# A fused attention and expert kernel: where the second expert unit's weights are split, and in which order

## The chip, the cores and the metric

The kernel runs as one program on one core of a Trainium2 chip. The metric is the time of one execution on the device in microseconds (us); lower is better. A core has engines that run side by side, each with its own queue of instructions: TensorE (PE, with its weight loads shown as PEld) multiplies matrices, VectorE (DVE) and ScalarE (ACT) work on elements, GpSimd (POOL) here issues indirect transfers, and SyncE (SP) issues most DMAs.

## The reference

The computation has three stages on 1792 tokens of width 768, all in 32-bit floats.

```python
attn = softmax(causal(q @ k.T / 8)) @ v          # 4 batches, 12 heads, 448 tokens, width 64
h = x @ w_in;  x = (h - tanh(h)) @ w_out         # 768 -> 2048 -> 768
logits = x @ w_gate;  e = argmax(logits)         # one of 8 experts for each token
for e in range(8):
    y = relu(x[mask_e] @ w1[e]) @ w2[e]          # 768 -> 1024 -> 768
    out[mask_e] = softmax_e * sigmoid(x @ w_output_gate[:, e]) * y
```

## The kernel before

Precision comes from splitting. A 32-bit operand is held as a high part, rounded by a cast on ACT (line 83), and a low part, the rest, by a subtraction on DVE (line 84); a product is then three TensorE products (high by high, low by high, high by low) that add up in PSUM.

The change lies in the third stage, `experts`. It works in units of 256 tokens of one expert: nine units, of which the first is the expert with the most tokens, the second is expert 0's ("early"), and the other seven follow. A unit of weights is 16 chunks of 128 x 768: eight for W1 and eight for W2. A unit runs eight *up* groups (`up`, lines 1098 to 1105: 18 products into one of three PSUM buffers named h, then a relu on ACT, line 1104, and the low part on DVE, line 1105) and four *down* groups (`down`, lines 1118 to 1127: 24 products for half of the tokens and half of the width, then a scaling on DVE or ACT). The tokens of the next unit are transposed and split inside a unit (`split`, lines 1086 to 1089: transposes on PE into tr, the cast xh on ACT, the rest xl on DVE).

Weights come in two steps. `Supply` (line 88) has eight rooms for raw chunks; SP fetches a chunk into a room (line 107) as soon as the room has been freed by the split of the chunk that stood there. `supply.load()` (line 111) splits the next raw chunk into a slot of the `ring` (class `Weights`, line 55). The ring has 16 slots, 18 once two spare ones have been added; a slot is free when the last product that reads it is done. During the last products of the second stage eight loads fill unit 0's W1. Each up group of a unit is followed by one load, and each down group by two. Unit 0 has two more at its end. So the sixteen loads of a unit run ahead of their use: in unit 0 the up groups are followed by the loads of its own W2, the down groups by those of unit 1's W1; from unit 1 on, two chunks further.

Unit 0 also carries the end of the routing: small steps (`late`) are taken from a list between its up groups, and the last of them, which make `allids` and `allcf`, in `leave()` behind the third down group. `leave()` then closes the routing's memory and opens the pool `ring2` in its place, with the two spare slots. `add_slots` puts them at the ring's present position, so the next two loads take them: in unit 0 these are the seventh and eighth chunk of unit 1's W1. Their splits have to wait until `allcf` has been made.

The order of instructions on an engine is not that of the program: a planner orders each engine's queue by its own model of costs, before the program runs. `tc.keep_in_program_order(x)` fixes one thing, that instruction x stands behind the instruction that was written just before it for the same engine; others can still be placed between. Once ordered, each queue runs in its order.

After the units a loop would take tokens of an expert beyond the planned ones. Whether it runs is in one word, `sel[0, 1]`, made in unit 0; `values_load` (line 1180) reads it into a register of each engine, and `tc.If` (line 1181) branches on it. With these inputs the loop does not run.

Of the kernel before, what the change touches and what calls it, by code (L numbers as in the profile page):

```python
# [9 lines left out]
F32 = mybir.dt.float32  # L10
# [4 lines left out]
ALU = mybir.AluOpType  # L15
# [39 lines left out]
class Weights:  # L55
# [20 lines left out]
    def unsplit(self, i):  # L76

        pool, n = self.slots[i]
        return pool.tile([P, 768, 2], I32, tag=f"w{n}", name=f"raw{n}", bufs=1)

    def split(self, raw, a):
        t = self.slot()
        self.nc.scalar.copy(t[:, 0, :], raw)  # L83
        self.nc.vector.tensor_tensor(t[:, 1, :], raw, t[:, 0, :].bitcast(F32), op=ALU.subtract)  # L84
        return self.parts(t, a)


# [34 lines left out]
class Decoder:  # L122
# [9 lines left out]
    keep = staticmethod(lambda x: x)  # L132
# [910 lines left out]
def gather(nc, pool, x2s, ids, c0):  # L1043

    xg = []
    for t in range(2):
        x = pool.tile([P, x2s.shape[1]], F32, tag="xg", name="xg")
        nc.gpsimd.indirect_dma_start(
            out=x, out_offset=None, in_=x2s,
            in_offset=IndirectOffsetOnAxis(ap=ids[:, c0 + t:c0 + t + 1], axis=0),  # L1050
        )
        xg.append(x)
    return xg
# [8 lines left out]
def experts(tc, consts, ring, xg, early, late, route_close, w12, x2s, lst, out):  # L1062


    nc = tc.nc
# [5 lines left out]
    supply = consts["supply"]  # L1071

    ctx = ExitStack()
    sp = ctx.enter_context(tc.tile_pool(name="ex", bufs=2))
    ps = consts["rtps"]
    rows = lst.rearrange("(r b) c -> r (b c)", b=P)

    def split(xg):
        hi = sp.tile([P, KD, 2, P], F32R, tag="xh", name="xh")
        lo = sp.tile([P, KD, 2, P], F32R, tag="xl", name="xl")  # L1080
        for k in range(KD // 2):
            pt = ps.tile([P, 2, 2, P], F32, tag="tr", name="tr")
            for a in range(2):
                for t in range(2):
                    d = (2 * k + a) * P
                    nc.tensor.transpose(pt[:, a, t, :], xg[t][:, d:d + P], ident)  # L1086
            s = slice(2 * k, 2 * k + 2)
            nc.scalar.copy(hi[:, s], pt)
            nc.vector.tensor_tensor(lo[:, s], pt, hi[:, s].bitcast(F32), op=ALU.subtract)
        return hi, lo  # L1090

    def up(x, w, f):
        ph = consts["hps"].tile([P, 2 * P], F32, tag="h", name="h")
        wh, wl = w
        n = 0
        for kd in range(KD):
            for wp, a in ((wh, x[0]), (wl, x[0]), (wh, x[1])):
                nc.tensor.matmul(  # L1098
                    ph, wp[:, kd, :], a[:, kd].rearrange("p a b -> p (a b)"),
                    start=(n == 0), stop=(n == 3 * KD - 1),  # L1100
                )
                n += 1
        h = [sp.tile([P, 2 * P], F32R, tag=f"h{i}", name=f"h{i}", bufs=KF) for i in range(2)]
        nc.scalar.activation(h[0], ph, AF.Relu)
        nc.vector.scalar_tensor_tensor(  # L1105
            h[1], ph, 0.0, h[0].bitcast(F32), op0=ALU.max, op1=ALU.subtract
        )
        return h

    def down(hs, W2, y, cf, t, o):  # L1110
        hn = DM // 2
        c = slice(t * P, (t + 1) * P)
        py = ps.tile([P, hn], F32, tag="y", name="py")
        n = 0
        for f in range(KF):
            wh, wl = W2[f]
            for a, w in ((0, wh), (0, wl), (1, wh)):
                nc.tensor.matmul(  # L1118
                    py, hs[f][a][:, c], w[:, 0, o * hn:(o + 1) * hn],
                    start=(n == 0), stop=(n == 3 * KF - 1),  # L1120
                )
                n += 1
        ye = y[:, o * hn:(o + 1) * hn]
        if o == 0:
            nc.vector.tensor_scalar_mul(ye, py, cf)
        else:
            nc.scalar.mul(ye, py, cf)

    def put(y, ids):
        nc.gpsimd.indirect_dma_start(  # L1130
            out=out, out_offset=IndirectOffsetOnAxis(ap=ids, axis=0),
            in_=y, in_offset=None, bounds_check=NT - 1, oob_is_err=False,
        )

    todo = [(consts[nm + "ids"], consts[nm + "cf"], 0) for nm in ("", "early")]
    todo += [(consts["allids"], consts["allcf"], 2 * e) for e in range(1, E)]
    x = split(xg)
    late.pop(0)()

    def leave():  # L1140

        nonlocal ps
        while late:
            late.pop(0)()
        route_close()
        rp = ctx.enter_context(tc.tile_pool(name="ring2", bufs=1))
        ring.add_slots(rp, 2)
        ps = ctx.enter_context(tc.tile_pool(name="exps", bufs=2, space=PSUM))

    for u, (iu, cu, c0) in enumerate(todo):  # L1150
        nxt = todo[u + 1] if u + 1 < len(todo) else None
        if u > 0 and nxt:
            xg = gather(nc, consts["xg"], x2s, nxt[0], nxt[2])
        hs = []
        W1 = supply.take(KF)
        for f in range(KF):
            hs.append(up(x, W1[f], f))
            supply.load()
            if u == 0:
                for _ in range(LATER[f]):  # L1160
                    late.pop(0)()
        if u == 0:
            xg = early[-1]
        W2 = supply.take(KF)
        for t in range(2):
            y = sp.tile([P, DM], F32, tag="y", name="y")
            for o in range(2):
                down(hs, W2, y, cu[:, c0 + t:c0 + t + 1], t, o)
                if (t, o) == ((1, 0) if u == 0 else (0, 0)) and nxt:
                    x = split(xg)  # L1170
                for _ in range(2):
                    supply.load()
                if u == 0 and (t, o) == (1, 0):
                    leave()
            put(y, iu[:, c0 + t:c0 + t + 1])
        if u == 0:
            for _ in range(2):
                supply.load()

    more = nc.values_load(consts["sel"][0:1, 1:2], min_val=0, max_val=1)  # L1180
    with tc.If(more > 0):
        for e in range(E):
            lo = nc.values_load(consts["begin"][0:1, e:e + 1], min_val=1, max_val=2)
            hi = nc.values_load(consts["units"][0:1, e:e + 1], min_val=0, max_val=per // 2)
            with tc.For_i(lo, hi, 1) as u:
                pt = turn_list(
                    nc, ps, fetch_list(nc, sp, rows[bass.ds(e * per + 2 * u, 2), :], 2), 2, ident
                )
                iu = sp.tile([P, 2], I32, tag="iu", name="iu", bufs=1)
                cu = sp.tile([P, 2], F32, tag="cu", name="cu", bufs=1)  # L1190
                nc.vector.tensor_copy(iu, pt[:, 0, :])
                nc.vector.tensor_copy(cu, pt[:, 1, :])
                x = split(gather(nc, consts["xg"], x2s, iu, 0))
                supply.add(weight_chunks(w12[e], KD, KF))
                supply.fill()
                for _ in range(2 * KF):
                    supply.load()
                W1, W2 = supply.take(KF), supply.take(KF)
                hs = [up(x, W1[f], f) for f in range(KF)]
                for t in range(2):  # L1200
                    y = sp.tile([P, DM], F32, tag="y", name="y")
                    for o in range(2):
                        down(hs, W2, y, cu[:, t:t + 1], t, o)
                    put(y, iu[:, t:t + 1])
# [4 lines left out]
def fused(ctx, tc, qk, v, w_in, w_out, gw, gates, w12, out):  # L1209
# [34 lines left out]
    def turnover():  # L1244
# [12 lines left out]
        tc, consts, ring, last, wo, gw, gates, w12, gT, x2s, lst  # L1257
    )
    experts(tc, consts, ring, xg, early, late, close, w12, x2s, lst, out)


# [61 lines left out]
```

## Time and profile before

| what | value |
| --- | --- |
| median of 3 runs | 1026.77 us (1023.33 to 1027.82) |
| profiled execution | 1028.09 us |
| its span | 1026.4 us, 16686 instructions |
| PE busy | 997.9 us, 97% of the span |
| DVE busy | 655.3 us, 64% |
| ACT busy | 489.0 us, 48% |
| POOL busy | 78.3 us, 8% |
| granted PE clock | 0.994 of full speed on average |
| up products of the experts (L1098) | 156.8 + 122.1 us |
| down products with the high part of h (L1118) | 155.3 us |
| weight casts (L83), expert stage | x144, 113.9 us |
| weight subtractions (L84), expert stage | x144, 131.7 us |
| fetches of expert weights (L107) | x144, 384 KB each, 5.2 us median to landing |

The span runs from the first instruction to the last of the profiled execution; its time on the device is 1.7 us longer. Attention and the two dense layers take the first two thirds; unit 0's first up product is at 689.5 us, and the last down product starts at 1013.9 us. Busy shares are averages over the whole span; idle time of an engine other than PE costs nothing unless PE waits for it.

### The profile page before, as it was taken

What the parts mean: (1) busy time and instruction counts of PE and PEld (TensorE: products, weight loads), DVE (VectorE), ACT (ScalarE), POOL (GpSimd) and SP (SyncE); (2) the same over time, 40 slices, a digit from 0 to 9 for tenths busy, and PEclk for the clock granted to TensorE, in tenths of its full rate; (3) what the DMA queues carried; (4) which work ended last, traced back from release to release, by engine and by line L of the source; (5) the groups of instructions that cost most, each with busy time, mean ns of one, the idle gap of its engine ahead of it and who ended that gap; (6) DMA issues with size and microseconds to landing.
All of it is one profiled execution on the core that took longest, in us unless ns stands there. A gap on an engine that the chain in (4) does not pass through costs nothing.

```text
span 1026.4 us, 16686 instructions
## 1 busy us (share of the span) xinstructions
PE 997.9 (97%) x6174; PEld 899.4 (88%) x6174; DVE 655.3 (64%) x1453; ACT 489.0 (48%) x1021; POOL 78.3 (8%) x84
## 2 busy tenths in 40 slices
PE   8999999999999999999999999999999999999995
PEld 3566888787878888999999999989999999999995
DVE  4779997877777745426677677556566654755530
ACT  4678886676766544312121122154554543554330
POOL 1000000000000000000111121111311111011000
PEclk9999999999999999999999999999999999999998
DMA  8444746675666318544242334298567755774500
GB/s 307 133 148 123 207 149 189 199 243 183 213 198 197 116 45 255 186 168 132 88 145 87 114 88 143 74 306 278 204 242 243 248 188 185 256 237 136 178 15 32
DMA packets 89100, 176.50 MB, mean 172 GB/s; under 512 B 8818, under 2 KB 52072, under 8 KB 89010
## 3 DMA queue, kind: packets, MB, share of 16 engines
q1 hardware_dynamic: 84258, 157.37, 48.3%
q0 software_dynamic: 4304, 16.97, 5.1%
q8 instruction: 50, 0.82, 0.4%
q10 hardware_dynamic: 448, 1.02, 0.3%
q14 instruction: 40, 0.33, 0.1%
HBM read 142.81 MB, written 34.08 MB: 172 GB/s over the span
## 4 chain that ended last, share of the span: by engine, by line
PE 78%; DMA 8%; DVE 7%; ACT 3%; issue 2%; SPq 0%; POOL 0%; POOLq 0%; ACTq 0%; DVEq 0%
PE x2p L683 20%; PE h L477 15%; PE h L1098 14%; PE py L1118 14%; DMA wo<-dy 3%; PE x L445 3%; PE pt L406 3%; PE s L341 3%; PE s L350 3%; DMA glo<-gT 2%; PE warm L506 2%; PE tr L1086 1%; DMA wraw<-in_w_dram 1%; DVE pr L367 1%; DVE w L84 1%
## 5 line engine op out<-in xcount | busy, mean ns | idle before, releaser
L477 PE MATMUL h<-xh,w 128*128 128x448 f32 x768 | 228.4, 375 | 0.8 <-DVE g L491 0.6
L683 PE MATMUL x2p<-w,ghi 128*128 128x384 f32 x896 | 228.9, 336 | 0.0
L683 PEld LDWEIGHTS x2p<-w,ghi 128*128 128x128 f32 x896 | 161.0, 188 | 0.3 <-issue 0.2
L1098 PE MATMUL h<-xh,w 128*128 128x256 f32 x864 | 156.8, 284 | 3.3 <-DVE h L1105 2.0
L1118 PE MATMUL py<-w,h 128*128 128x384 f32 x864 | 155.3, 336 | 0.0
L683 PE MATMUL x2p<-w,glo 128*128 128x384 f32 x448 | 150.0, 335 | 0.0
L1118 PEld LDWEIGHTS py<-w,h 128*128 128x128 f32 x864 | 149.1, 188 | 0.0
L477 PEld LDWEIGHTS h<-xh,w 128*128 128x128 f32 x768 | 139.2, 189 | 10.0 <-DVE g L491 1.4
L84 DVE TENSOR_TENSOR w<-wraw,w 128x768 fp32r<-128x768 f32 x144 | 131.7, 953 | 21.5 <-ACT w L83 21.5
L477 PE MATMUL h<-xl,w 128*128 128x448 f32 x384 | 142.4, 373 | 0.0
L1098 PEld LDWEIGHTS h<-xh,w 128*128 128x128 f32 x864 | 134.7, 191 | 4.3 <-DVE h L1105 2.2
L83 ACT CAST w<-wraw 128x768 fp32r<-128x768 f32 x144 | 113.9, 830 | 36.1 <-PE py L1118 28.5
L1098 PE MATMUL h<-xl,w 128*128 128x256 f32 x432 | 122.1, 283 | 0.0
L376 ACT ACTIVATE pr<-pr,mx 128x128 f32<-128x128 f32 (+3 forms) x168 | 89.0, 530 | 52.8 <-DVE mx L367 49.3
L706 DVE CUSTOM_DVE_ANT_0 junk<-x,row 128x768 bf16<-128x768 f32 x88 | 84.2, 957 | 31.8 <-ACT x L692 29.6
L683 PEld LDWEIGHTS x2p<-w,glo 128*128 128x128 f32 x448 | 84.1, 188 | 0.2 <-issue 0.2
L1098 PEld LDWEIGHTS h<-xl,w 128*128 128x128 f32 x432 | 82.6, 191 | 0.4 <-issue 0.4
L367 DVE CUSTOM_DVE_ANT_0 pr<-s,mask 128x384 f32<-128x384 f32 (+2 forms) x144 | 60.1, 420 | 30.9 <-PE s L341 20.4
L477 PEld LDWEIGHTS h<-xl,w 128*128 128x128 f32 x384 | 72.3, 189 | 4.6
L406 PE MATMUL pt<-ident,pr 128*128 128x128 f32 x384 | 62.7, 276 | 0.2 <-ACT pr L389 0.2
L491 DVE TENSOR_TENSOR g<-h,g 128x448 f32<-128x448 f32 x64 | 39.6, 620 | 34.6 <-ACT g L490 34.2
L406 PEld LDWEIGHTS pt<-ident,pr 128*128 128x128 f32 x384 | 46.5, 141 | 13.5 <-issue 4.1
(178 smaller groups left out, 1174.9 us busy)
## 6 DMA issues: line engine op xcount, KB each, us to landing
wraw<-in_w_dram SPq DMA_DIRECT2D x144, 384.0 KB, 5.2
gT<-g SPq DMA_DIRECT2D x64, 224.0 KB, 2.2
glo<-gT SPq DMA_DIRECT2D x14, 1024.0 KB, 7.2
draw<-in_w_out_dram SPq DMA_DIRECT2D x16, 768.0 KB, 4.8
raw<-in_w_in_dram SPq DMA_DIRECT2D x14, 768.0 KB, 6.1
q<-in_qk_dram SPq DMA_DIRECT2D x36, 240.0 KB, 3.9
k<-in_qk_dram SPq DMA_DIRECT2D x36, 224.0 KB, 3.9
wo<-dy SPq DMA_DIRECT2D x16, 384.0 KB, 4.6
```

Source lines behind the costliest of these rows:

```text
L83: self.nc.scalar.copy(t[:, 0, :], raw)
L84: self.nc.vector.tensor_tensor(t[:, 1, :], raw, t[:, 0, :].bitcast(F32), op=ALU.subtract)
L341: nc.tensor.matmul(d, self.qh[:, o:o + P], x[:, kcol[i]:kcol[i] + w], start=(n == 0), stop=(n == last - 1),)
L367: nc.vector.tensor_tensor_reduce(out=self.probs(r), in0=ss[:, o:o + w], in1=m, scale=-0.125, scalar=3.0e38, op0=ALU.add, op1=ALU.min, accu ...
L376: nc.scalar.activation(pc, pc, AF.Exp, bias=self.mx[:, x:x + 1], scale=-1.0, accum_out=self.sm[:, x:x + 1],)
L406: nc.tensor.transpose(pt[:, n * P:(n + 1) * P], self.pr[:, o:o + P], ident)
L477: nc.tensor.matmul(ph, w[:, kd, :], x, start=(kd == 0 and n == 0), stop=(kd == KD - 1 and n == 2))
L491: nc.vector.tensor_tensor(g, ph, g, op=ALU.subtract)
L683: nc.tensor.matmul(px, a[:, f, :], w[:, 0, h * hn:(h + 1) * hn], start=(n == 0), stop=(n == 3 * NF - 1),)
L706: nc.vector.tensor_tensor_reduce(out=junk, in0=x2, in1=row, scale=1.0, scalar=0.0, op0=ALU.mult, op1=ALU.add, accum_out=to,)
L1098: nc.tensor.matmul(ph, wp[:, kd, :], a[:, kd].rearrange("p a b -> p (a b)"), start=(n == 0), stop=(n == 3 * KD - 1),)
L1118: nc.tensor.matmul(py, hs[f][a][:, c], w[:, 0, o * hn:(o + 1) * hn], start=(n == 0), stop=(n == 3 * KF - 1),)
```

## The change

There are four edits. (1) `Weights` gets a hook `keep`, and both instructions of a weight split pass through it. In units 0 and 1 it is set to `tc.keep_in_program_order` after the first up group and set back when the unit's W2 is taken, so the splits written between the up groups of these two units are pinned behind the relu and the h subtraction of the group before them. (2) The loads in the down part stand ahead of each down group instead of behind it; in unit 0 they are four ahead of each of the first two groups and none ahead of the others, where it was two behind each of four. (3) The spare slots are added to the ring after unit 0's last down group instead of in `leave()`; the pool is still opened there. So all eight W1 chunks of unit 1 take slots of unit 0's W1, and the two spare slots go to the first two chunks of unit 1's W2. (4) The word for the loop is read at the beginning of the last unit instead of behind it.

```diff
+    keep = staticmethod(lambda x: x)
+
     def split(self, raw, a):
         t = self.slot()
-        self.nc.scalar.copy(t[:, 0, :], raw)
-        self.nc.vector.tensor_tensor(t[:, 1, :], raw, t[:, 0, :].bitcast(F32), op=ALU.subtract)
+        self.keep(self.nc.scalar.copy(t[:, 0, :], raw))
+        self.keep(self.nc.vector.tensor_tensor(
+            t[:, 1, :], raw, t[:, 0, :].bitcast(F32), op=ALU.subtract
+        ))
         return self.parts(t, a)
...
         route_close()
-        rp = ctx.enter_context(tc.tile_pool(name="ring2", bufs=1))
-        ring.add_slots(rp, 2)
+        ring2 = ctx.enter_context(tc.tile_pool(name="ring2", bufs=1))
         ps = ctx.enter_context(tc.tile_pool(name="exps", bufs=2, space=PSUM))
 
     for u, (iu, cu, c0) in enumerate(todo):
+        if u == len(todo) - 1:
+            more = nc.values_load(consts["sel"][0:1, 1:2], min_val=0, max_val=1)
...
         for f in range(KF):
             hs.append(up(x, W1[f], f))
+            if u < 2:
+                ring.keep = tc.keep_in_program_order
             supply.load()
...
         W2 = supply.take(KF)
+        ring.keep = lambda x: x
         for t in range(2):
             y = sp.tile([P, DM], F32, tag="y", name="y")
             for o in range(2):
+
+                for _ in range(2 if u else 4 - 4 * t):
+                    supply.load()
                 down(hs, W2, y, cu[:, c0 + t:c0 + t + 1], t, o)
                 if (t, o) == ((1, 0) if u == 0 else (0, 0)) and nxt:
                     x = split(xg)
-                for _ in range(2):
-                    supply.load()
                 if u == 0 and (t, o) == (1, 0):
                     leave()
             put(y, iu[:, c0 + t:c0 + t + 1])
         if u == 0:
+            ring.add_slots(ring2, 2)
             for _ in range(2):
                 supply.load()
 
-    more = nc.values_load(consts["sel"][0:1, 1:2], min_val=0, max_val=1)
     with tc.If(more > 0):
```

## Rows read from the trace of the kernel before

**Rows 1.** Windows: stretch, busy us of PE, PEld, DVE, ACT, POOL; clock; DMA.
```profile
686.00:712.00 26.00, 24.06 (x200) 22.50 (x199) 22.46 (x59) 16.70 (x34) 3.81 (x4) 1.00 0.90 278
743.10:745.40 2.30, 0.29 (x4) 0.09 (x2) 0.49 (x2) 1.62 (x3) 0.00 (x0) 1.00 1.05 413
```

**Rows 2.** Waits of PE, 640 to 1026 us: total, times, longest.
```profile
PE h L1098 <- DVE h L1105: 2.0, 1, 2.0
PE h L1098 <- ACT xh L1088: 1.3, 2, 1.1
PE tr L1086 <- DVE xl L1089: 0.9, 1, 0.9
```

**Rows 3.** Timeline of PE, unit 0's start: start, length, instruction, idle before.
```profile
687.77 0.63 PE L734 MATMUL lg<-x2T,gw 128*32 128x256 f32 x6
689.48 0.97 PE L1098 MATMUL h<-xh,w 128*128 128x256 f32 x6 [1.08 <-ACT xh L1088]
691.30 0.66 PE L1086 MATMUL tr<-ident,xg 128*128 128x128 f32 x4 [0.85 <-DVE xl L1089]
```

**Rows 4.** Timelines of ACT and DVE before and at unit 0's start.
```profile
678.80 8.41 ACT L83 CAST w<-wraw 128x768 fp32r<-128x768 f32 x11 [0.57 <-PE x2p L683]
687.11 0.47 ACT L692 COPY x<-x2p 128x384 f32<-128x384 f32 x1
688.85 1.07 ACT L1088 CAST xh<-tr 128x512 fp32r<-128x512 f32 x2
...
679.67 2.70 DVE L84 TENSOR_TENSOR w<-wraw,w 128x768 fp32r<-128x768 f32 x3 [1.04 <-ACT w L83]
682.75 7.90 DVE L84 TENSOR_TENSOR w<-wraw,w 128x768 fp32r<-128x768 f32 x9
690.57 1.28 DVE L1089 TENSOR_TENSOR xl<-tr,xh 128x512 fp32r<-128x512 f32 x2
```

**Rows 5.** Timeline of ACT, unit 1's up groups.
```profile
728.21 4.52 ACT L83 CAST w<-wraw 128x768 fp32r<-128x768 f32 x6 [1.26 <-DVE allcf L977]
...
737.80 2.31 ACT L83 CAST w<-wraw 128x768 fp32r<-128x768 f32 x3 [2.39 <-DMA wraw<-in_w_dram]
...
743.76 0.83 ACT L83 CAST w<-wraw 128x768 fp32r<-128x768 f32 x1 [1.31 <-DMA wraw<-in_w_dram]
744.50 0.38 ACT L1104 ACTIVATE h<-h 128x256 fp32r<-128x256 f32 x1
```

**Rows 6.** Waits of all engines, 700 to 760 us, ACT's for weights.
```profile
ACT w L83 <- DMA wraw<-in_w_dram: 4.9, 3, 2.4
```

**Rows 7.** DMA issues, 727 to 745 us: count, size, median us to landing.
```profile
wraw<-in_w_dram SPq DMA_DIRECT2D x11, 384.0 KB, 8.0
```

**Rows 8.** Line 107, all 144 weight fetches: issue to landing.
```profile
DMA to landing us min/median/max: 2.8/5.2/10.2
```

**Rows 9.** Timelines of ACT, DVE and PE, unit 0's change from up to down.
```profile
711.66 0.83 ACT L83 CAST w<-wraw 128x768 fp32r<-128x768 f32 x1
...
712.52 0.96 DVE L84 TENSOR_TENSOR w<-wraw,w 128x768 fp32r<-128x768 f32 x1 [0.30 <-ACT w L83]
...
711.18 12.65 PE L1118 MATMUL py<-w,h 128*128 128x384 f32 x72
```

**Rows 10.** Chain that ended last, unit 2's up groups: start, length.
```profile
767.91 17.27 PE h L1098 x144
```

**Rows 11.** Line 1180, the loop's word: ns min/median/max, first and last start.
```profile
L1180 PEldq TENSOR_LOAD <-sel x1: 487/487/487, 1010.9 to 1010.9; - x1
...
L1180 POOLq TENSOR_LOAD <-sel x1: 305/305/305, 1014.9 to 1014.9; - x1
```

**Rows 12.** Tile h, the down products, first and last start.
```profile
L1118 PE MATMUL py<-w,h x864: 331/334/429, 711.2 to 1013.9; 128*128 128x384 f32 x173
```

**Rows 13.** Line 1181, POOL's waits behind the branch, first and last start.
```profile
L1181 POOLq EVENT_SEMAPHORE  x5: 17/43/43, 1018.3 to 1018.7; - x5
```

**Rows 14.** Line 1130, the last two puts: issue to landing.
```profile
DMA to landing us min/median/max: 3.0/3.3/3.5
```

More of the change, by code (lines that the diff above doesn't have):

```diff
@@ L1138, in experts @@
     late.pop(0)()
+    ring2 = None
     def leave():
-        nonlocal ps
+        nonlocal ps, ring2
         while late:
```

## The prediction

> **What bounds the kernel now.** I read the page's engine shares first: TensorE is busy 97% of the span, so a change can only win where TensorE stands still or where the end hangs on something else. Second, the windows by stage: in the stretch of the first expert unit (686 to 712 us) PE is busy 24.06 of 26.00 us, and between 743.1 and 745.4 us, inside the second unit's up products, 0.29 of 2.30 us [rows 1]. Third, the waits of PE from 640 us to the end: 2.0 us once on DVE's h, 1.3 us in two waits on ACT's xh, 0.9 us once on DVE's xl, and nothing else that falls into the expert units [rows 2]. These are all that the expert stage has to give: 2.0 + 1.3 + 0.9 = 4.2 us of standing PE.
>
> **Stall 1, the start of the first unit.** PE ends six lg products near 688.4 us, waits 1.08 us for ACT's xh and, after six up products, 0.85 us for DVE's xl [rows 3]. What holds ACT and DVE is in their timelines: ACT runs 11 weight casts in one row from 678.80 us and comes to xh at 688.85 us; DVE runs 3 and then 9 weight subtractions and comes to xl only at 690.57 us [rows 4]. The first unit needs eight W1 chunks at its start; the ninth cast and the later ones are its W2, wanted only by the down products from 711 us.
>
> **Stall 2, the second unit.** Near 728 us ACT, freed by allcf, runs 6 casts in a row, which empties the rooms that hold raw weights. The refills then come late: the casts at 737.80 and 743.76 us wait 2.39 and 1.31 us for a DMA, and the relu at 744.50 us stands behind such a cast in ACT's order [rows 5]; three such waits make 4.9 us [rows 6]. The DMAs of this stretch landed in a median of 8.0 us, against 5.2 us over all [rows 7, 8]. Three PSUM buffers absorb part of the 4.9 us; 2.0 us reach PE.
>
> **The change, part by part.**
> Pinning in unit 0: the eight splits of its W2, each an ACT cast and a DVE subtraction, go behind the relu and the subtraction of the up product of the same number. So ACT has 8 casts ahead of xh: 8 x 0.765 us (8.41 us for 11) from 678.80 ends at 684.9 us. xh then starts behind the x copy (687.11 + 0.47 = 687.6 us), and the first of the two (1.07 us) is done near 688.2 us, before the lg products end at 688.4 us: 1.08 us gone. DVE's first 8 subtractions end at 682.75 + 5 x 0.878 = 687.1 us (7.90 us for 9), so xl follows xh by some 0.7 us (1.28 us for two) at 688.9 us; six up products, 0.97 us from 688.4, end at 689.4 us, later than that: 0.85 us gone [rows 3, 4]. What is late next is the third transposed part, which has the other up products beside it, as now. Gain 1.93 us; bounds 0 (another filler takes the place) and 1.93.
>
> The price of it: W2's eighth chunk is now split behind the eighth relu. That place holds a cast and a subtraction already, at 711.66 and 712.52 us, so the chunk would be ready at 713.5 us. The first down group starts at 711.18 us with 72 products in 12.65 us, 0.1735 us each; the chunk's low half is read by product 23, at 711.18 + 22 x 0.1735 = 715.0 us [rows 9]. Slack 1.5 us. One cast of the second unit's W1 slipped in between costs 0.83 us on ACT and 0.96 us on DVE and still fits; two would cost PE 0.4 us. I take 0, with 0.4 as the upper bound.
>
> Loads of unit 1's W1: four ahead of each of the first two down groups, all eight into slots of unit 0's W1, and none behind. In the old order six went there and two waited for the new slots until allcf; those two now go out late, to unit 1's W2. Each chunk's raw data is fetched when a pinned subtraction frees a room, one per up product, so the eight DMAs come 2.16 us apart (17.27 us for 144 products, eight up products [rows 10]) instead of 0.88 us. SP issues the same DMAs in the same sequence; no gather or list of POOL's gets a new wait. Unit 1 starts near 728 us, over 10 us after its last W1 cast could run. Cost 0; the bounds are C below and 0.
>
> Pinning in unit 1: at its start the rooms hold all eight W2 chunks. Two splits can run after allcf as now; the six others follow relus 0 to 5, so none of these relus stands behind a cast without data, and the refills are issued over some 13 us (6 x 2.16). Gain 2.0 us; bounds 0 and 2.0. I take 2.0, because the pinned casts' data is in the rooms before the unit begins. What is late next: unpinned casts of unit 2's W1, with refills 5.2 us away, against 4.3 us that two spare PSUM buffers cover (2 x 2.16) besides the relu's own distance.
>
> Loads ahead of each down group instead of behind it in units 1 to 8: the same casts, one group earlier in the program. They wait for slots that products free, which does not change, and PE does not stand in units 2 to 8 [rows 2]. I take 0. Bounds: -0.2 us (the smaller of the two xh waits, which is at the second unit's start), and +1.1 us a unit, the length of the larger xh wait, if a cast came to stand ahead of xh.
>
> The loop's word: each queue reads it once. PE's read takes 0.487 us, POOL's 0.305 us [rows 11]. On PE it will stand among products instead of behind them. PE's queue read it at 1010.9 us while products started until 1013.9 us [rows 12], so the queue was 3 us ahead of the array: hidden, 0; if it is not ahead, 0.49 us. At the end, the last put goes out beside POOL's read at 1014.9 us and lands 3.0 to 3.5 us later; POOL's waits begin at 1018.3 us and end at 1018.7 us [rows 13, 14]: the branch and the landing end together, so an earlier read gives 0, at most its own 0.3 us. I take 0 for both. The Trainium skill's "DMA: Bandwidth & Descriptors" (Latency and other measured facts) states a floor of about 600 ns for such a load; the trace has less, 487 and 305 ns, so the trace decides. By the page, and unhidden, the sum below would be 0.6 us smaller, an estimate from that page.
>
> Sum: -1.93 - 2.0 = -3.9 us. The profiled execution took 1028.09 us (span 1026.4 and 1.7 around it): 1024.2 us. It lies 1.3 us above the median of the runs, 1026.77, and on that scale the forecast is **1022.8 us**. PE's clock adds nothing: the granted clock is 1.00 in the 2.30 us around the stall [rows 1].
>
> **Rivals.**
> A, both stalls go: 1022.8 us, 0.60.
> B, only one goes, because the planner fills the freed place at the first unit's start with other work, or unpinned casts still block a relu in the second: -2.0, 1024.8 us; 0.20. For it: a pin fixes what a split follows, not what may slip between.
> C, slower: the wait for DMA moves into unit 0. A room there is freed only by a pinned subtraction, and the eight W1 casts of unit 1 are unpinned; if the planner places some before their data lands, ACT stops in front of relu 7 and of the last W2 cast. With the 4.9 us of ACT waits now seen in unit 1 [rows 6], less the slack of 1.5, PE loses 3.4 us, and unit 1 keeps its 2.0: -1.93 + 3.4 = +1.5 us, 1028.3 us. It decides from an ACT wait of 1.5 + 1.93 = 3.4 us. Against it: the fetches are spread, and the quickest landing is 2.8 us [rows 8]. 0.10.
> The Trainium skill's "Perfetto Trace Analysis" (Per-engine timelines, Tensor Engine Instruction) says that ACT's queue is strictly first in, first out; by that rule a pin cannot protect a relu from an unpinned cast that stands ahead of it, and the relu at 744.50 us behind its late cast agrees [rows 5].
> D, the pins change the order little and the stalls stay: 1026.8 us; 0.10. Against it: 11 casts in a row before xh are plainly not the pinned order.
>
> **How the numbers follow.** About 0.5%, 5.1 us, is the smallest difference that a measurement of this kernel can tell from no change. All standing time of PE in the stage is 4.2 us, so faster by more than that needs the scatter of the runs (1023.33 to 1027.82) on top of A: 0.3 of A and 0.1 of B, together 0.20. Slower needs C at several times its price: 0.05. Same: 0.75. A alone, with the scatter: 1020.5 to 1025. The range takes in B, D and most of C's way to 1028.3: 1019.8 to 1027.8 us.
>
> **What would show it.** Right: PE's waits on xh and xl near 688 us are gone and ACT has 8 weight casts before xh; in unit 0 each W2 cast follows its relu; PE's wait on DVE's h in unit 1 is gone, and no ACT cast waits 2 us or more for DMA after 728 us. Wrong: a new PE wait on w in the first down group near 715 us (the price of pinning, or C), an up product that waits on h in unit 0, PE standing where it reads the word in the last unit, or idle PE in units 2 to 8.

## The result, and the profile after

The changed kernel takes 1032.70 us (median of 18 runs, 1029.79 to 1040.09) against 1027.28 us for the kernel before (18 runs, 1023.33 to 1031.25): slower by 5.4 us. The ratio on record, 1.0059 with a 95% interval of 1.0043 to 1.0075, is not exactly the quotient of the two medians; it stands for 6.1 us (4.4 to 7.7). The forecast was 1022.8 us, with 1027.8 us as its upper end. The profiled execution took 1031.4 us (span 1029.7).

In the changed code the cast of a weight is line 86 (83 before), its subtraction 87, the fetch 112, the up products 1103, relu and h subtraction 1109 and 1110, the transposes 1091, xh and xl 1093 and 1094, the down products 1123.

First view, the waits of PE from 640 us to the end in the kernel after (total, times, longest), which answers to [rows 2]:

```profile
PE py L1123 <- ACT w L86: 3.7, 1, 3.7
PE g L755 <- ACT lgT L745: 2.8, 1, 2.8
PE tr L1091 <- DVE xl L1094: 2.4, 1, 2.4
PE py L1123 <- DVE w L87: 0.5, 1, 0.5
PE py L1123 <- DVE h L1110: 0.5, 1, 0.5
PE py L1123 <- ACT h L1109: 0.5, 1, 0.5
PE h L1103 <- ACT xh L1093: 0.2, 1, 0.2
```

The waits of before on xh, xl and h are gone (the 0.2 us is the smaller xh wait that was there already). In their place stand, in unit 0, down products (py) that wait for weights, 4.2 us, and in unit 1 down products that wait for h, 1.0 us, and transposes (tr) that wait for xl, 2.4 us. The 2.8 us on lgT lies ahead of unit 0, at 654 us, in the routing.

What I had forecast for unit 0's start did come. Timelines of PE and ACT there, to hold against [rows 3, 4]:

```profile
684.97 0.63 PE L739 MATMUL lg<-x2T,gw 128*32 128x256 f32 x6
685.72 0.98 PE L1103 MATMUL h<-xh,w 128*128 128x256 f32 x6
686.54 0.60 PE L1091 MATMUL tr<-ident,xg 128*128 128x128 f32 x4
...
676.01 5.99 ACT L86 CAST w<-wraw 128x768 fp32r<-128x768 f32 x8 [0.57 <-DMA wraw<-in_w_dram]
685.08 1.07 ACT L1093 CAST xh<-tr 128x512 fp32r<-128x512 f32 x2 [0.40 <-PE tr L1091]
```

ACT has eight casts in a row instead of eleven, and PE goes from lg to h and tr without a stop. The loss comes at the other end of unit 0, where the up groups give way to the down groups. Timelines of ACT, DVE and PE, to hold against [rows 9]:

```profile
704.62 0.38 ACT L1109 ACTIVATE h<-h 128x256 fp32r<-128x256 f32 x1
704.90 0.82 ACT L86 CAST w<-wraw 128x768 fp32r<-128x768 f32 x1
711.98 0.83 ACT L86 CAST w<-wraw 128x768 fp32r<-128x768 f32 x1 [6.26 <-DMA wraw<-in_w_dram]
712.72 0.38 ACT L1109 ACTIVATE h<-h 128x256 fp32r<-128x256 f32 x1
713.00 0.82 ACT L86 CAST w<-wraw 128x768 fp32r<-128x768 f32 x1
...
713.85 1.83 DVE L87 TENSOR_TENSOR w<-wraw,w 128x768 fp32r<-128x768 f32 x2 [0.30 <-ACT w L86]
...
706.37 3.81 PE L1123 MATMUL py<-w,h 128*128 128x384 f32 x21
713.87 0.45 PE L1123 MATMUL py<-w,h 128*128 128x384 f32 x1 [3.69 <-ACT w L86]
714.86 10.32 PE L1123 MATMUL py<-w,h 128*128 128x384 f32 x50 [0.55 <-DVE w L87]
```

The reader is to see the order on ACT: the seventh relu, the seventh cast of W2, then at 711.98 us a cast of unit 1's W1 that waits 6.26 us for its data, and only behind it the eighth relu and the eighth cast of W2. PE runs 21 products, stands 3.69 and 0.55 us for that cast and its subtraction, and then takes 10.32 us for 50 products, where [rows 9] has 0.1757 us for each (12.65 us for 72), 8.8 us. The window (busy us of PE, PEld, DVE, ACT, POOL; clock; DMA share, GB/s) gives the reason for the last 1.5 us, a granted clock of 0.72, between its two levels of 1.2 and 2.4 GHz:

```profile
713.90:720.00 6.10, 5.55 (x23) 5.29 (x24) 3.65 (x5) 1.67 (x2) 0.64 (x1) 0.72 0.99 280
```

The late data: first the seven fetches of line 112 issued between 700 and 709 us, to hold against [rows 8]; then POOL's DMAs in that time (count, median us to landing), and the window of 704 to 708 us; last the three fetches that the kernel before issued at about the same time, at 699.0 to 703.7 us.

```profile
L112 SPq DMA_DIRECT2D wraw<-in_w_dram x7: 327/328/331, 701.9 to 708.1; - x7
...
DMA to landing us min/median/max: 9.0/10.8/11.5
```

```profile
lst<-pr,sl POOLq DMA_INDIRECT x2, 8.4
xg<-x2s,earlyids POOLq DMA_INDIRECT x2, 10.4
```

```profile
704.00:708.00 4.00, 4.00 (x32) 4.00 (x31) 3.89 (x6) 1.72 (x3) 0.34 (x1) 1.00 0.73 57
```

```profile
DMA to landing us min/median/max: 3.0/4.1/5.5
```

The DMA engines are 73% busy between 704 and 708 us and move 57 GB/s. In that time POOL's list send (lst, its first part issued at 698.4 us) and early gather (xg, 700.5 and 701.8 us) are under way. Three of the seven fetches are unit 1's W1, those of 702.8, 705.0 and 707.2 us, for which the casts at 711.98, 715.51 and 718.74 us wait; the other four are already its W2. Before, all eight fetches of unit 1's W1 were issued from 688.1 to 695.9 us and landed in 6.4 to 7.9 us, ahead of the send at 704.3 us; the three fetches of the last fence, of W2, had landed by 706.7 us. So two things moved: counted from unit 0's first up product, the seventh W1 fetch went from 5.6 us to 21.5 us, and the send went out earlier, at 12.7 us instead of 14.8.

In unit 1 the same pattern shows on ACT, to hold against [rows 5]; two of the PE lines that pay for it stand below. (The relu that the first of them waits for starts at 752.82 us, behind casts of which one, at 750.11 us, had waited 2.63 us for its data.)

```profile
756.97 0.83 ACT L86 CAST w<-wraw 128x768 fp32r<-128x768 f32 x1 [2.09 <-DMA wraw<-in_w_dram]
757.71 1.06 ACT L1093 CAST xh<-tr 128x512 fp32r<-128x512 f32 x2
760.24 0.84 ACT L86 CAST w<-wraw 128x768 fp32r<-128x768 f32 x1 [1.47 <-DMA wraw<-in_w_dram]
...
753.25 0.62 PE L1123 MATMUL py<-w,h 128*128 128x384 f32 x2 [0.48 <-ACT h L1109]
759.45 0.66 PE L1091 MATMUL tr<-ident,xg 128*128 128x128 f32 x4 [2.35 <-DVE xl L1094]
```

From 700 to 760 us ACT waits 19.3 us for weights, in eight waits; before it was 4.9 us in three [rows 6]:

```profile
ACT w L86 <- DMA wraw<-in_w_dram: 19.3, 8, 6.3
```

To compare kernels without the scatter of earlier stages I measure two stretches on PE's timeline: unit 0, from the end of the last lg product ahead of its first up product to unit 1's first up product, and unit 1, from there to unit 2's first up product. Idle is PE's, gaps over 0.2 us. Medians and ratios are of repeated runs (18 of after, 6 of e6, 8 each of e8 to e10, 12 each of the others), the stretches of the one profiled execution of each kernel. The kernel before, run beside each set, had medians of 1027.41 us (e1 to e4), 1026.72 us (e5 to e8) and 1027.43 us (e9 to e12).

| kernel | unit 0 (idle) | unit 1 (idle) | both | median us | ratio to before |
| --- | --- | --- | --- | --- | --- |
| before | 36.54 (2.18) | 42.80 (2.01) | 79.35 | 1027.28 | |
| after | 40.69 (4.48) | 44.80 (3.36) | 85.48 | 1032.70 | 1.0059 [1.0043, 1.0075] |
| e1, pins in unit 0 | 40.02 (3.82) | 43.04 (2.02) | 83.06 | 1030.99 | 1.0044 [1.0024, 1.0064] |
| e2, pins in unit 1 | 36.76 (2.10) | 45.54 (2.47) | 82.30 | 1029.25 | 1.0018 [1.0001, 1.0035] |
| e3, no pins | 36.54 (2.16) | 43.10 (2.09) | 79.64 | 1028.06 | 1.0008 [0.9985, 1.0030] |
| e4, unit 0's pins longer | 34.51 (0.24) | 46.10 (2.88) | 80.61 | 1026.53 | 0.9994 [0.9973, 1.0015] |
| e5, as e4, none in unit 1 | 34.51 (0.24) | 43.28 (2.25) | 77.79 | 1022.31 | 0.9961 [0.9945, 0.9978] |
| e6, both units' longer | 34.51 (0.24) | 40.77 (0.00) | 75.28 | 1019.58 | 0.9934 [0.9907, 0.9960] |
| e7, pins alone | 41.56 (3.81) | 44.91 (3.50) | 86.47 | 1030.16 | 1.0030 [1.0012, 1.0048] |
| e8, after, no last send | 36.89 (2.07) | 46.61 (3.23) | 83.50 | 1027.68 | 1.0011 [0.9991, 1.0031] |
| e9, after, no early gather | 39.83 (3.45) | 45.95 (2.92) | 85.79 | 1029.58 | 1.0006 [0.9978, 1.0034] |
| e10, after, neither | 34.52 (0.24) | 45.15 (3.49) | 79.67 | 1023.58 | 0.9964 [0.9939, 0.9989] |
| e11, longer pins alone | 35.05 (0.77) | 42.82 (0.66) | 77.87 | 1023.62 | 0.9960 [0.9934, 0.9987] |
| e12, e6 again | 34.51 (0.24) | 40.77 (0.00) | 75.28 | 1022.19 | 0.9944 [0.9923, 0.9965] |

The change costs 4.15 us in unit 0 and 2.00 us in unit 1, 6.1 us in all, against 5.4 us in the medians: the two stretches hold the result. Where PE waits no more than 0.24 us, unit 0 takes 34.51 us and unit 1 40.77 us; so the kernel before lost 2.03 + 2.03 us there, and the changed one 6.18 + 4.03 us.

### The profile page after: what moved, and what is told of

Its sections match the earlier page's. It is cut to its first block, busy times and chain, and to the rows that moved or that the text cites. A ratio compares the mean times of both kernels' runs of the same rounds, so it can differ in the third digit from the quotient of the medians.

```text
span 1029.7 us, 16659 instructions
## 1 busy us (share of the span) xinstructions
PE 999.0 (97%) x6174; PEld 899.8 (87%) x6174; DVE 656.6 (64%) x1453; ACT 488.8 (47%) x1021; POOL 78.4 (8%) x84
## 4 chain that ended last, share of the span: by engine, by line
PE 82%; DMA 7%; DVE 6%; ACT 3%; issue 2%; SPq 0%; POOL 0%; POOLq 0%; ACTq 0%; DVEq 0%
PE x2p L688 22%; PE h L482 17%; PE py L1123 13%; PE h L1103 13%; PE x L450 3%; PE pt L411 3%; PE s L346 3%; DMA wo<-dy 3%; PE s L355 3%; DMA wraw<-in_w_dram 2%; PE warm L511 2%; PE tr L1091 1%; DVE pr L372 1%; DVE w L87 1%; DMA glo<-gT 1%
## 5 line engine op out<-in xcount | busy, mean ns | idle before, releaser
L1123 PE MATMUL py<-w,h 128*128 128x384 f32 x864 | 157.8, 339 | 5.2 <-ACT w L86 3.7
L496 DVE TENSOR_TENSOR g<-h,g 128x448 f32<-128x448 f32 x64 | 39.7, 622 | 34.5 <-ACT g L495 34.3
```

The source lines that it names most:

```text
L496: nc.vector.tensor_tensor(g, ph, g, op=ALU.subtract)
L1123: nc.tensor.matmul(py, hs[f][a][:, c], w[:, 0, o * hn:(o + 1) * hn], start=(n == 0), stop=(n == 3 * KF - 1),)
```

## The experiments

Theory T, in short: the pins themselves cost nothing, but they free the rooms later, so that the fetches of the next unit's W1 fall where data arrives late, and the planner has put the unpinned casts of these chunks ahead of work that PE needs. The rivals: a pinned W2 chunk is late by itself (R1); another edit does it (R2).

### Which edit: e1, e2, e3, e7

```diff
-            if u < 2:
+            if u < 1:        # e1;  e2: u == 1;  e3: u < 0
                 ring.keep = tc.keep_in_program_order
```

> Pins kept in unit 0 only. Theory T (the pins move the fetches of unit 1's W1 so late that casts without data stand in ACT's order ahead of relu 7 and of the last W2 cast of unit 0): the start of unit 0 without its two waits (-1.9 us), in unit 0's first down group a PE wait of about 4.2 us and some 1.5 us at a lower granted clock behind it, unit 1 as in the kernel before (one wait of about 2.0 us on h). Sum -1.9 + 4.2 + 1.5 = +3.8 us against the kernel before, near 1031 us. Rival R1 (a pinned W2 chunk is late by itself, whatever unit 1's loads do): the same time, but ACT shows no DMA wait ahead of the last W2 cast. Rival R2 (loads ahead of the down groups and the late spare slots cost the time): also 1031 us or more, and the kernel without pins as slow.

> Pins kept in unit 1 only. T: unit 0 as in the kernel before (waits of 1.1 and 0.9 us at its start, none in its down groups), unit 1 as in the changed kernel: 3.4 us of PE waits in its down part (0.5 + 0.5 + 2.4) in place of the 2.0 us in its up part, so +1.4 us against the kernel before, near 1028.7 us. If my forecast for unit 1 had been right by itself and was only spoilt by what unit 0 left behind: -2.0 us, near 1025.3 us, and no wait in unit 1.

> The changed kernel without any pin: loads ahead of the down groups, late spare slots and early word are left. T: as the kernel before within 1 us (near 1027.3 us), waits of 1.1 and 0.9 us at unit 0's start, about 2.0 us in unit 1, none in unit 0's down groups. R2 (the loads or the slots cost the time): 3 us or more above the kernel before, with the new wait in unit 0's first down group.

Each came near its number: 1030.99, 1029.25 and 1028.06 us (expected by T: 1031, 1028.7, 1027.3). In e1 unit 0 has the new wait and unit 1 the old one; PE's waits in e1:

```profile
PE py L1123 <- ACT w L86: 3.0, 1, 3.0
PE h L1103 <- DVE h L1110: 2.0, 1, 2.0
```

e2 is the mirror of it: unit 0 36.76 us as before, unit 1 45.54 us, 2.7 us worse than before. That is more than the 1.4 us of T, and the waits lie elsewhere than in the changed kernel: 1.78 and 0.43 us on h in the first down group, none on xl. So my forecast for unit 1 was wrong by itself, not spoilt by unit 0. e3 is not to be told from the kernel before: R2 falls. The other half of that question, the pins without the other three edits:

```diff
 (kernel before)
+    keep = staticmethod(lambda x: x)
 ...
+            if u < 2:
+                ring.keep = tc.keep_in_program_order
             supply.load()
 ...
         W2 = supply.take(KF)
+        ring.keep = lambda x: x
```

> The kernel before with the pins alone (both units, as in the change); loads behind the down groups, spare slots handed out early, word read late, as before. T: the pins are the whole of the change's effect: as the changed kernel, +5.4 us, near 1032.7 us, with a wait of about 4 us in unit 0's first down group. If moving the loads ahead of the down groups is needed for the loss (they put the casts of unit 1's W1 earlier in the program): less than +3 us, and no ACT cast of unit 1's W1 ahead of relu 7.

It (e7) has the same wait at the same place, 3.27 + 0.30 us, and 86.47 us for the two units against 85.48, so the pins are the whole effect in them. Its median is only 3.4 us above before, 2 us short of what I expected, with an interval that overlaps the changed kernel's; whether the other edits cost a little outside the two units is left open. I had thought that the loads ahead of the down groups might be needed for the loss; they are not.

### Is it the pinned W2 or what is slipped between: e4

```diff
         W2 = supply.take(KF)
-        ring.keep = lambda x: x
+        if u:
+            ring.keep = lambda x: x
 ...
         if u == 0:
+            ring.keep = lambda x: x
             ring.add_slots(ring2, 2)
```

> The pins of unit 0 are kept on over its down part too, so that unit 1's W1 casts stand behind relu 7 and the last W2 cast in ACT's order; unit 1 as in the changed kernel. T: the fetches of unit 1's W1 are as late as before, but ACT waits for them where PE wants nothing of it: the wait in unit 0's first down group goes from 4.2 us to 0.4 or less and with it the lower clock, the start of unit 0 keeps its -1.9 us, unit 1 its +1.4 us or more. Sum about -0.5 us, near 1026.8 us, some 5 us under the changed kernel. R1 (the pinned W2 is late by itself): the wait stays at 3 us or more, near 1031 us.

Unit 0 falls to 34.51 us, with no wait in its down groups. Its W2 is pinned as in the change, so R1 falls. ACT in e4, around the same place:

```profile
706.39 0.38 ACT L1109 ACTIVATE h<-h 128x256 fp32r<-128x256 f32 x1 [1.05 <-PE h L1103]
706.67 4.50 ACT L86 CAST w<-wraw 128x768 fp32r<-128x768 f32 x6
713.47 2.31 ACT L86 CAST w<-wraw 128x768 fp32r<-128x768 f32 x3 [2.30 <-DMA wraw<-in_w_dram]
```

The eighth relu is on time, the eighth W2 cast is the first of the six behind it, and the casts of unit 1's W1 wait behind both, where nobody needs ACT. Unit 1 got worse than in the change, 46.10 us; so e4 as a whole is level with the kernel before. That 46.10 us holds 2.88 us of waits, and PE's clock behind them, from 753 to 757 us, was 0.62.

### What makes the data late: e8, e9, e10

```diff
-            then = [(2, route.logits), (p - 2, route.choose), (p, route.place), (p, route.send)]
+            then = [(2, route.logits), (p - 2, route.choose), (p, route.place)]
+            then += [(p, route.send if t0 < LATE else lambda: None)]             # e8, e10
 ...
-        early.append(gather(nc, consts["xg"], x2s, consts["earlyids"], 0))
+        early.append(first[2])                                                   # e9, e10
```

> The changed kernel without the sending of the last token group's list rows, so that the later units' lists lack those tokens; pins and the order of ACT as in the changed kernel. If this send makes the stretch in which all DMA queues stand (702 to 708 us): the fetches of unit 1's W1 issued there land in 3 to 5 us instead of 9 to 11.5, and the wait in unit 0's first down group falls from 4.2 us to 1 us or less. If it is the early gather of unit 1's tokens, or only the number of fetches in flight: landings and wait stay as they are (9 us or more, over 3 us).

> The changed kernel without the early gather of unit 1's tokens (unit 1 takes unit 0's tokens); the last list send stays, ACT's order as in the changed kernel. e8, without the send, landed the late fetches in 4.3 to 6.5 us instead of 9 to 11.5 and cut the wait in unit 0's first down group from 4.2 to 1.8 us. If the send alone makes the slow stretch: landings of 8 us or more and a wait of 3 us or more. If both small transfers share it: landings of 5 to 8 us and a wait of 1 to 3 us, as in e8.

> The changed kernel without the last list send and without the early gather (the later units' lists lack the last tokens, unit 1 takes unit 0's). T says the pinned order hurts only as far as the fetches land late: with both gone they should land in 3 to 4 us as the pinned ones before 700 us do, and the wait in unit 0's first down group should be 0.5 us or less though ACT's order is that of the changed kernel. If the order alone is enough (casts of unit 1's W1 ahead of relu 7 by their own 0.8 us each): 1 us or more stays.

The window of 704 to 708 us in e8, e9 and e10, one fence each:

```profile
704.00:708.00 4.00, 4.00 (x27) 4.00 (x26) 2.21 (x3) 0.22 (x1) 0.00 (x0) 1.00 0.98 321
```

```profile
704.00:708.00 4.00, 4.00 (x34) 4.00 (x34) 4.00 (x7) 2.25 (x4) 0.00 (x0) 1.00 1.05 58
```

```profile
704.00:708.00 4.00, 4.00 (x29) 4.00 (x28) 3.70 (x6) 2.38 (x4) 0.00 (x0) 1.00 0.95 296
```

The DMA queues from 700 to 709 us (packets, MB, share of 16 engines) and the fetches issued in that time, in e9 and then in e10 (SP's fetches are in q1, the send in q0):

```profile
q1 hardware_dynamic: 269, 0.74, 75.5%
...
q0 software_dynamic: 32, 0.00, 0.2%
...
wraw<-in_w_dram SPq DMA_DIRECT2D x8, 384.0 KB, 8.0
```

```profile
q1 hardware_dynamic: 848, 2.32, 83.4%
...
wraw<-in_w_dram SPq DMA_DIRECT2D x8, 384.0 KB, 5.1
```

The send alone (e9) makes the hole: 58 GB/s, against 321 GB/s with the gather alone (e8). Its own 32 packets take 0.2% of the DMA engines' time; it is the fetches' packets that take longer with it, 0.40 us each on average (75.5% of 16 engines for 9 us, over 269) instead of 0.14 us (83.4%, 848). Each run was profiled once, but five other profiles with the send (after, e2, e3, e7, e11) have 48 to 59 GB/s in the same window. Why the packets take longer is not shown. Median landings: 10.8 us with both transfers, 8.0 with the send, 6.3 with the gather (e8), 5.1 with neither; the wait in unit 0's first down group: 4.24, 3.21, 1.83 and 0 us. By its own cases e9 fell, narrowly, on the side of the send alone (8.0 us, over 3 us), while e8's 1.83 us without the send lay between its two cases; I read the four together as both sharing it, the send the more. I had expected 3 to 4 us of landing in e10 and got a median of 5.1; that the fetches still follow one another quickly may be why, but was not tested. The wait went to nothing with ACT's order unchanged:

```profile
705.69 0.84 ACT L86 CAST w<-wraw 128x768 fp32r<-128x768 f32 x1 [1.15 <-DMA wraw<-in_w_dram]
706.44 0.38 ACT L1110 ACTIVATE h<-h 128x256 fp32r<-128x256 f32 x1
706.71 0.83 ACT L86 CAST w<-wraw 128x768 fp32r<-128x768 f32 x1
```

The same cast stands ahead of the eighth relu; it waits 1.15 us instead of 6.26, and that fits into the slack. With e4 this shows T from both sides: good order with late data (e4), and bad order with earlier data (e10), each bring unit 0 to 34.5 us. The totals of e8 to e10 hold less work than the kernel's and prove nothing more.

### A version that beats both: e5, e6, e11, e12

```diff
-            if u < 2:                            # e5: pins of e4, unit 0 alone
+            if u < 1:
 ...
         W2 = supply.take(KF)                     # e6, e12: both units, whole unit
-        ring.keep = lambda x: x
+        if u > 1:
+            ring.keep = lambda x: x
 ...
             put(y, iu[:, c0 + t:c0 + t + 1])
+        ring.keep = lambda x: x
```

> Pins in unit 0 alone, kept on over its down part; none in unit 1. From the last lg product to unit 1's first up product the runs so far took 36.5 us (kernel before), 40.6 (changed kernel), 34.4 (e4); unit 1 took 42.8 us without pins, 44.8 to 46.1 with them. T (each unit's order prices itself): unit 0 as in e4, unit 1 as before, with its one wait of about 2.0 us: -2.1 us, near 1025.3 us. Rival (what was gained in unit 0 comes back in unit 1, whose casts now follow later fetches): unit 1 takes 44 us or more, and the time is that of the kernel before.

> Pins in both units, each kept on over the unit's down part too, so that in unit 1 six of the eight casts of unit 2's W1 stand behind its last relu and behind the xh copies. T: unit 0 as in e4 (-2.1 us); in unit 1 no cast that waits for data stands ahead of a relu or of xh, so the 2.0 us wait of the kernel before goes and nothing takes its place: about 40.8 us for unit 1. Sum -4.1 us, near 1023.2 us, what I had forecast for the change. Rival (in unit 1 the pinned splits are late by themselves, since its W2 comes late): 1 us or more of PE waits on w or h in unit 1's down part and a time of 1025 us or more.

> The kernel before with the pins of both units kept on over their down parts, and nothing else of the change: loads behind the down groups, spare slots early, word late. If the other three edits do nothing even here: the time of e6 within 2 us, both units without a wait over 0.3 us. If the loads ahead of the down groups matter once the pins are longer (behind a group a kept split also follows that group's place in program order): a later W1 of the next unit, with PE waits on w or xh at the start of unit 1 or 2, and a time 2 us or more above e6.

> e6 once more, on the chip that runs e11, to narrow its interval. By the stage alone (75.2 us from unit 0's last lg product to unit 2 against 79.4 in the kernel before) -4.2 us, near 1022.7 us; e6's median was 7 us under the kernel before. If the longer pins also gain outside the stage: 1021 us or less again, with a span outside the stage clearly under 944 us.

e6 and e12 are the same program; e11 has its pins on the kernel before. e5 and e6 did what T said of the units: 34.51 us in unit 0, 43.28 us in unit 1 of e5 (42.80 before, the rival's 44 not reached), and in e6 and e12 no waits in unit 1 either. PE's waits from 640 us in e12, and ACT at the end of unit 1:

```profile
PE g L755 <- ACT lgT L745: 0.5, 1, 0.5
PE h L1103 <- ACT xh L1093: 0.2, 1, 0.2
```

```profile
741.47 0.39 ACT L1109 ACTIVATE h<-h 128x256 fp32r<-128x256 f32 x1 [1.05 <-PE h L1103]
741.75 2.29 ACT L86 CAST w<-wraw 128x768 fp32r<-128x768 f32 x3
746.10 1.07 ACT L1093 CAST xh<-tr 128x512 fp32r<-128x512 f32 x2 [2.05 <-PE tr L1091]
```

ACT waits for PE there, not PE for ACT. In the two units e6 is 4.07 us faster than the kernel before, which is the 3.9 us that I had forecast for the change itself. The medians are lower by more, 7.1 us in e6 and 5.2 us in e12, both faster than before beyond their intervals; 4.1 us lies at the edge of the one interval (4.1 to 9.6 us) and well inside the other (3.6 to 7.9 us). e5 has the same excess: T said 1025.3 us, the median was 1022.3, 4.4 us under before where the units give 1.6. The spans of e6 and e12 differ by 3.7 us with the same 75.28 us in the units; outside the two units their profiles take 946.2 and 942.5 us, that of before 947.1, so single profiles can't say whether the rest is a gain or scatter. e12's median lies between its two cases. That stays open.

In e11, without the other three edits, a pinned cast with late data (1.36 us of waiting at 716.96 us) stands ahead of unit 1's xh copies, PE waits 0.77 and 0.66 us, and a lower clock follows. It is 1.4 us slower than e12 in the medians, with overlapping intervals, and 2.6 us in the two units, in one profile each. I take the place of the loads to be the edit that the longer pins need; no run gives the loads and the spare slots one by one, so this is argued and not shown.

## Why the prediction was wrong

**Stall 1, -1.93 us: right.** Both waits went, for the reason given on DVE's side. On ACT's side the row of eleven casts was not what PE waited for: it had ended when the x copy of 687.11 us began. Between that copy and xh stood a twelfth cast, and it had waited for its data:

```profile
688.11 0.83 ACT L83 CAST w<-wraw 128x768 fp32r<-128x768 f32 x1 [0.53 <-DMA wraw<-in_w_dram]
```

So the mechanism of the later loss, a cast without data ahead of what PE needs, was in this stall already. In the runs where nothing else was in the way (e4 to e6) unit 0 gained 2.03 us.

**The price of pinning in unit 0, taken as 0: this step failed.** For the pinned chunk itself 0 was right (e4). The failure is in the sentence "One cast of the second unit's W1 slipped in between costs 0.83 us on ACT and 0.96 us on DVE and still fits". I priced a slipped cast by its own length and not by when its data comes: the wait ahead of it was 6.26 us, and 4.24 us of that reached PE. I had set against it that the fetches are spread, and used the quickest landing, 2.8 us [rows 8]; here they took 9.0 to 11.5 us, where 10.2 us was the slowest of before. In the trace of before the send at 704 us and its slow stretch were there to be read (from 706 to 712 us the DMA engines are 69% busy and move 39 GB/s); I did not put the new times of the fetches over it.

**Loads of unit 1's W1, cost 0: failed with it.** The spread came about as forecast (691.5, 694.3, 696.6, 699.4, 702.8, 705.0 and 707.2 us), and it is what carried the fetches into the send. "The same DMAs in the same sequence" was not so: from 701.9 us on, fetches of unit 1's W2 go out between those of its W1. And the send itself came earlier, which the text had not reckoned with.

**Rival C was the mechanism**, with a chance of 0.10: a wait for DMA that moves into unit 0 ahead of relu 7 and of the last W2 cast, with PE waiting on w near 715 us, which the text named as the sign. Its size was off: 3.4 us priced, 4.24 us measured, and behind it 1.94 us more (6.18 - 4.24) that it had not counted, the lower clock; and it left unit 1 as before, where 2.0 us were lost besides. The rule cited there, the Trainium skill's "Perfetto Trace Analysis" (Per-engine timelines, Tensor Engine Instruction), that ACT's queue is strictly first in, first out, agrees with the trace: the eighth relu starts at 712.72 us, when the late cast ahead of it has run, though the last up product, its input, had ended near 706.5 us.

**PE's clock "adds nothing": failed.** I read it off one stall of 2.0 us at 1.00 [rows 1]. After 3.69 + 0.55 us it was 0.72 for 6.1 us.

**Pinning in unit 1, -2.0 us: failed.** The wait on h in the up groups went, as forecast; e2 has 0.26 us of it left. But the unpinned casts of unit 2's weights took the place at the end of the unit, ahead of the last relus and the xh copies. I had named those of its W1 as "what is late next", set their 5.2 us against 4.3 us of cover, and still priced them at nothing. "The pinned casts' data is in the rooms" was true of the pinned ones alone. The cost was +2.0 us instead of -2.0; e6 gives the -2.0 once these casts are pinned too.

**Loads ahead of the down groups: 0 was right** for the change (e3), and no PE wait shows in units 2 to 8. **The word: 0 was right, but its reasons were not put to the test.** The reads of the word in the kernel after, to hold against [rows 11]:

```profile
L1157 PEldq TENSOR_LOAD <-sel x1: 487/487/487, 1014.1 to 1014.1; - x1
...
L1157 POOLq TENSOR_LOAD <-sel x1: 306/306/306, 1018.1 to 1018.1; - x1
```

PE's read stands 15.6 us and POOL's 11.6 us before the end of the span; before it was 15.5 and 11.5 us. The edit moved the read in the program, but neither queue came to it any earlier, so whether an earlier read would be hidden was not seen.

The sum by what was measured: unit 0 -2.03 + 6.18 = +4.15, unit 1 +2.00, together +6.1 us where I had -3.9.

## What to carry to other kernels

A pin on one kind of work leaves the planner free to put another kind in front of it, and on an in-order engine a cast that waits for its data costs whatever stands behind it: here the pins paid once they held through the whole unit, and cost time when they held through half of it. Price a slipped instruction by the landing of its data at its new time, and lay the new issue times over every slow stretch of the old trace. An engine may wait for data without cost, as ACT did in e4 (2.30 us), if what PE needs stands ahead of the wait.

## What the runs showed of the hardware

With an indirect send of 32 packets, 0.2% of the DMA engines' time, the core moved 58 GB/s for some 4 us, without it 296 (e9, e10): packets of other transfers took 0.40 us on average instead of 0.14.

A PE stall costs its length and sometimes a lower granted clock behind it, and the length alone did not tell which: 2.25 us in e5 left 1.00, and 0.77 + 0.66 us in e11 were followed by 0.63.

```profile
739.00:743.00 4.00, 3.87 (x32) 3.87 (x33) 4.00 (x7) 3.46 (x7) 0.00 (x0) 1.00 0.99 366
```

```profile
721.00:724.00 3.00, 3.00 (x16) 2.81 (x17) 2.36 (x8) 2.05 (x3) 0.00 (x0) 0.63 0.65 247
```

The first fence is e5, from the end of its wait; the second e11.
